# Moving gathered token rows into a quartered tile by sixteen transfers between partitions, without a copy in DRAM

## The chip, the cores and the metric

One Trainium2 chip, one of its cores. The metric is the device time of one execution in microseconds; the median of three runs of the kernel before is 671.84 us (670.88 to 672.2). Smaller is better. The engines are TensorE (PE in the profile; its weight loads stand apart as PEld), VectorE (DVE), ScalarE (ACT), GpSimd (POOL) and SyncE (SP), which here only issues transfers. A "q" behind an engine's name (SPq, DVEq) means its instruction queue: waits, branches and transfer issues.

## What is computed

Two layers one behind the other, all in 32-bit floats. The first is a linear attention with random features over 8 batches, 8 heads, 576 positions and 64 channels. Its output, 4608 rows of 512 values, goes through a mixture of experts in which each row is served by one of 8 experts:

```python
logits = x @ w_gate
expert_idx = np.argmax(logits, axis=1)
gate_w = probs[np.arange(N), expert_idx]      # probs: softmax of logits
for e in range(E):
    mask = expert_idx == e
    h = np.maximum(x[mask] @ w1[e], 0.0)      # 512 -> 1024
    out[mask] = gate_w[mask, None] * (h @ w2[e])   # 1024 -> 512
```

## The kernel before

Up to about 255 us the attention runs; it writes its rows, with the gate's weight behind each, to a DRAM tensor `token_rows`, and the routing (class `Routing`) makes index lists that sort the rows by expert. What follows is class `Experts`: it serves the sorted rows in chunks of up to 448 (three tiles of 128 rows and one of 64) that belong to one expert. The chunk in hand is counted by t. A first, early part of 256 rows is served before chunk 0. In this execution chunks 0 to 11 hold rows; moves and gathers are made for one or two more.

A step (`step`, line 1190) of chunk t consists of

- `layer1(t)`: four groups of two hidden blocks. Each group has 24 matmuls on TensorE, 96 in the chunk (line 1034), then `high_low` (line 1048): ScalarE makes the high part of the hidden block (line 1049), VectorE the low part (line 1050). Two PSUM buffers serve the four groups in turn, so the third group waits until VectorE has read the first.
- `layer2(t)`: up to 72 matmuls (line 932) or 16 for a half tile (line 1069) that make the output rows. Which tiles are done depends on the row count of the chunk, by branches in the instruction streams (`either`, line 1120; `three`, line 1108).
- `weigh(t+1)` and `gather(t+3)`: GpSimd copies the gate weights (line 981) and gathers the rows of a later chunk from `token_rows` into `xg[(t+3) % 2]`, four indirect transfers (line 975).
- `begin(t+1)` (line 1178): the move of chunk t+2 on SyncE, then the weight fetches if the expert changes (w2 at line 952, w1 at line 949, 2 MB each, both on SyncE), the split of w1 in a high and a low part on ScalarE (line 61) and VectorE (line 55), and `xrows(t+2)` (line 1013).
- `out2`: ScalarE scales the output rows (line 1151), GpSimd scatters them (line 1131).

The order on each engine is that of the code: it is scheduled by hand. Only at t = 1 `xrows(2)` stands within `layer1` (line 1091). In a step with a new expert `layer1` also splits w2, two blocks before each group.

The change is in `move` (line 989). The rows of a chunk lie in `xg`, one row on a partition. TensorE needs them turned. VectorE's transpose (line 1003) works on blocks of 32 by 32 within 32 partitions, so the columns must first be dealt out: the tile `xq` has in its q-th 32 partitions the q-th 128 columns of all rows, 32 rows to a block. `move` makes it by way of DRAM: two stores (lines 993 and 994) of 768 KB and 128 KB into `chunk_rows`, and four loads (line 996) of 224 KB, one for each quarter of the partitions, in pieces of 512 bytes. There is one `xq` and there are two `chunk_rows`; so the loads wait for the four transposes of the move before, and the stores don't. `xtrans` (line 998) writes the turned rows back into `xg`, `part` (line 1007) makes the high part on ScalarE (line 1010) and the low part on VectorE (line 55).

The framework sets the semaphores for all of this. A transfer that SyncE issues gets one of eight completion semaphores, in turn; the transfer that comes to a semaphore again waits for the one before on it.

In the profile the twelve moves are counted 1 to 12; move 1 is issued before chunk 0 starts.

Of the kernel before, what the change touches and what calls it, by code (L numbers as in the profile page):

```python
# [10 lines left out]
F32 = mybir.dt.float32  # L11
# [9 lines left out]
P = 128  # L21
Q = 32
B, H, S, D, M = 8, 8, 576, 64, 128
DM = H * D
# [12 lines left out]
A3 = 3  # L37
T3 = A3 * P
HT = P // 2
T4 = T3 + HT  # L40
# [795 lines left out]
class Experts:  # L836
# [7 lines left out]
    def __init__(self, tc, ctx, rt, xs, w1, w2, out, ident, ps):  # L844
        self.tc, self.nc, self.ctx, self.rt, self.ps, self.ident = tc, tc.nc, ctx, rt, ps, ident
        self.xs, self.w1, self.w2 = xs, w1, w2

        self.out = dram_disjoint_views(out, A3 + 1)
        cp = ctx.enter_context(tc.tile_pool(name="mo_a", bufs=1))
        self.w1s = cp.tile([P, self.NC, F], F32, name="w1s")  # L850
        self.w2s = cp.tile([P, self.NF, DM], F32, name="w2s")
        self.idx = cp.tile([P, NS], U32, name="idx")
        self.idx0 = cp.tile([P, 2], U32, name="idx0")
        self.flags = cp.tile([1, 5, NQ], I32, name="flags")
        self.xg = [cp.tile([P, A3 + 1, ROW], F32, name="xg")]
        self.clear = lambda: self.nc.gpsimd.memset(self.xg[0], 0.0)
        rt.setup()
        *rt.after[3], last = rt.head(4, self.idx0, self.flags)
        rt.late[5] = [last]
        self.x0 = cp.tile([P, self.NC, self.T2], F32, name="x0")  # L860
        self.bounce = [self.nc.dram_tensor(f"chunk_rows{i}", (T4, DM), F32, kind="Internal").ap() for i in range(2)]
        gt = cp.tile([P, 4 + 2 * A3], F32, name="gt")
        self.gt = [gt[:, i:i + 1] for i in range(4 + 2 * A3)]
        self.stored, self.now = 0, SimpleNamespace(r2=None, r3=None, fetch=None)
# [124 lines left out]
    def move(self, t):  # L989


        rows, x, dma = self.bounce[t % 2], self.xg[t % 2], self.nc.sync.dma_start
        dma(rows[:T3].rearrange("(a p) n -> p a n", p=P), x[:, :A3, :DM])
        dma(rows[T3:], x[:HT, A3, :DM])
        for q in range(4):
            dma(self.xq[q * Q:(q + 1) * Q], rows[:, q * P:(q + 1) * P].rearrange("(g i) n -> i g n", i=Q))

    def xtrans(self, t, a):

# [319 lines left out]
```

## Time and profile before

| | |
|---|---|
| median of three runs | 671.84 us (670.88 to 672.2) |
| the profiled execution, its own time | 675.24 us |
| its span, first to last instruction | 673.4 us |
| mean granted TensorE clock over the span | 0.991 of full speed |
| attention, from the span's start | to about 255 us |
| chunks 0 to 11 (TensorE, line 1034 and 932) | 268.1 to 666.1 us |

The profile is of one execution. "Busy" is time in which an engine computes; waits, branches and transfer issues don't count. A timeline lists start, duration, engine, line, operation, the tiles written and read, and in brackets how long the engine was idle before and what ended that. "remote" and "issue" there mean that no semaphore of this program's engines was found that ended the idle time.

### The profile page before, as it was taken

To read this page: it belongs to the slowest core of one execution; us is meant where nothing else is said; L and a number is where in the kernel's file an instruction comes from. 1 tells how busy PE (TensorE), PEld (TensorE's weight loads), DVE (VectorE), ACT (ScalarE), POOL (GpSimd) and SP (SyncE) were. 2 spreads that over 40 slices of the span, in tenths; PEclk is the share of its full clock that TensorE was granted. 3 is DMA by queue.
4 is the path that set the end of the run, shared out by engine and by line. 5 is a ranking of instruction groups with operands and counts; after the bars stand their busy time and mean duration, and the time that the engine had idled before them with its cause. 6 is when DMAs were issued, how large, how long until landed. Compare 5 with 4: busy or idle time off the path is not lost. (4 is left out here: it accounts for less than half of the span.)

```text
span 673.4 us, 19200 instructions
## 1 busy us (share of the span) xinstructions
PE 653.0 (97%) x6979; PEld 591.0 (88%) x6979; DVE 375.3 (56%) x755; ACT 359.8 (53%) x1089; POOL 280.5 (42%) x514
## 2 busy tenths in 40 slices
PE   8999999999999999999999999999997999999995
PEld 5999999999989987989898989898987989898984
DVE  4788888888888787732524184323267064614110
ACT  4999999999999956422222163212244143413111
POOL 5645546887788775152241304121222304031302
PEclk8999999999999999999999999999998999999998
DMA  7863926638390533759774256843268718530101
GB/s 216 230 186 105 278 84 202 192 104 263 77 336 27 181 103 85 200 167 308 186 195 83 84 159 151 251 127 87 67 216 215 217 53 230 197 91 18 35 1 56
DMA packets 95531, 102.07 MB, mean 152 GB/s; under 512 B 29454, under 2 KB 75534, under 8 KB 94736
## 3 DMA queue, kind: packets, MB, share of 16 engines
q1 hardware_dynamic: 87248, 80.84, 41.4%
q0 software_dynamic: 7440, 19.04, 9.3%
q8 instruction: 92, 1.51, 1.0%
q14 instruction: 63, 0.52, 0.3%
q10 hardware_dynamic: 688, 0.16, 0.1%
HBM read 74.77 MB, written 30.43 MB: 156 GB/s over the span
## 5 line engine op out<-in xcount | busy, mean ns | idle before, releaser
L1034 PE MATMUL p<-xb,w1p 128*128 128x384 f32 (+3 forms) x1152 | 195.8, 329 | 2.0 <-DVE hb L1050 1.9
L1034 PEld LDWEIGHTS p<-xb,w1p 128*128 128x128 f32 x1152 | 191.5, 188 | 5.9 <-DVE hb L1050 2.5
L932 PE MATMUL p<-w2p,hb 128*128 128x512 f32 x792 | 183.5, 392 | 3.6 <-PEq L1109 3.6
L932 PEld LDWEIGHTS p<-w2p,hb 128*128 128x128 f32 x792 | 149.6, 189 | 34.8 <-issue 3.8
L1131 POOL DMA_INDIRECT out_dram<-ys,idx x38 | 38.2, 1004 | 278.8 <-DVEq L1121 135.8
L1050 DVE SCALAR_TENSOR_TENSOR hb<-p,hb 128x768 fp32r<-128x768 f32 (+1 forms) x48 | 42.7, 890 | 191.5 <-ACT hb L1049 138.1
L1049 ACT ACTIVATE hb<-p 128x768 fp32r<-128x768 f32 (+1 forms) x48 | 36.4, 758 | 124.0 <-PE p L1034 92.3
L195 DVE TENSOR_REDUCE mx<-pp 128x8 f32<-128x1024 f32 x64 | 78.0, 1218 | 10.8 <-PE pp L189 9.0
L203 ACT ACTIVATE qp<-pp,mx 128x128 f32<-128x128 f32 x256 | 76.8, 432 | 0.0
L203 ACT ACTIVATE kp<-pp,mx 128x128 f32<-128x128 f32 x256 | 73.8, 382 | 5.2 <-DVE de L287 1.3
L189 PE MATMUL pp<-omt,th 64*128 64x128 f32 x1024 | 71.6, 280 | 0.2 <-ACT qp_-1_323 L203 0.2
L189 PEld LDWEIGHTS pp<-omt,th 64*128 64x128 f32 x1024 | 63.0, 190 | 0.3 <-ACT qp_-1_323 L203 0.3
L215 POOL TENSOR_TENSOR k<-kp 128x256 f32<-128x256 f32 x64 | 46.5, 726 | 25.2 <-ACT kp L203 19.5
L1151 ACT ACTIVATE ys<-p,gt 128x512 f32<-128x512 f32 x30 | 20.6, 688 | 59.0 <-PE p L932 36.6
L180 DVE COPY th<-tr 128x512 f32<-128x512 f32 x63 | 43.3, 687 | 6.1 <-PE tr L172 4.2
L278 PE MATMUL nu<-kva,qt 128*64 128x73 f32 x1008 | 46.0, 233 | 0.0
L247 ACT COPY qt<-t 128x512 f32<-128x512 f32 x64 | 41.8, 653 | 2.2 <-PE t L172 1.8
L975 POOL DMA_INDIRECT xg<-token_rows,idx x31 | 32.0, 1032 | 21.4 <-DVE xb L55 7.9
L278 PEld LDWEIGHTS nu<-kva,qt 128*64 128x64 f32 x1008 | 36.7, 136 | 4.2
L229 PE MATMUL kf<-kp,v 128*64 128x128 f32 x512 | 39.7, 275 | 0.4 <-issue 0.4
L975 POOL DMA_INDIRECT xgm<-token_rows,idx x28 | 28.2, 1008 | 7.6 <-issue 6.7
L216 POOL TENSOR_TENSOR ks<-k 128x128 f32<-128x128 f32 x64 | 29.2, 457 | 5.0
(382 smaller groups left out, 945.5 us busy)
## 6 DMA issues: line engine op xcount, KB each, us to landing
xq<-chunk_rows SPq DMA_DIRECT2D x48, 224.0 KB
w1s<-in_moe_w_dram SPq DMA_DIRECT2D x5, 2048.0 KB
w2s<-in_moe_w_dram SPq DMA_DIRECT2D x5, 2048.0 KB
v<-in_v_dram SPq DMA_DIRECT2D x32, 256.0 KB
token_rows<-x SPq DMA_DIRECT2D x8, 1024.0 KB
k<-in_k_dram SPq DMA_DIRECT2D x31, 256.0 KB
q<-in_q_dram SPq DMA_DIRECT2D x31, 256.0 KB
chunk_rows<-xgm SPq DMA_DIRECT2D x6, 768.0 KB
```

The lines of the kernel that those rows point to most:

```text
L180: self.nc.vector.tensor_copy(t.rearrange("p n (a t) -> p a n t", a=2), s[("tr", h)])
L189: nc.tensor.matmul(o[:, a, n, :], t[r, n, :], self.om[r], start=True, stop=True)
L195: self.nc.vector.tensor_reduce(out=mx, in_=s[("pp", h)], axis=AX.X, op=ALU.max, negate=True)
L203: self.nc.scalar.activation(o[:, j, :], p[:, a, 2 * n + i, :], AF.Exp, bias=mx[:, a, 2 * n + i:2 * n + i + 1])
L215: nc.gpsimd.tensor_tensor(out=k2, in0=kp[:, :2, :], in1=kp[:, 2:, :], op=ALU.add)
L229: nc.tensor.matmul(pkv[c * D:(c + 1) * D, :M], vv, kk, start=n < 2, stop=n > 2)
L247: self.nc.scalar.copy(qt.rearrange("p n (a t) -> p a n t", a=2), s[("t2", h)])
L278: nc.tensor.matmul(o[r, j, :], qt[:, j, r], kva[:, h if h >= 0 else 2 * j + a, :], start=True, stop=True)
L932: self.nc.tensor.matmul(p, x, w[:, c, :], start=c == 0 and x is h and w is self.w2h, stop=c == self.NF - 1 and x is l)
L975: self.nc.gpsimd.indirect_dma_start(out=self.xg[t % 2][:self.span(a), a, :], out_offset=None, in_=self.xs[:, :], in_offset=bass.IndirectOf ...
L1034: self.nc.tensor.matmul(o, w[:, c, k], x[:, c, :], start=i == 0, stop=i == len(ops) - 1)
L1050: self.nc.vector.scalar_tensor_tensor(out=l, in0=p, scalar=0.0, in1=h.bitcast(F32), op0=ALU.max, op1=ALU.subtract)
```

## The change

The two DRAM tensors go, and with them the two stores. In place of the four loads there are sixteen transfers from `xg` to `xq`, one for each 32 partitions g and each quarter of the columns q. Each takes the 32 partitions g of the source, of every row tile that has them (four tiles for g = 0 and 1, with the half tile; three for g = 2 and 3), and writes 32 partitions q, every fourth block. They are of 64 KB or 48 KB, again in pieces of 512 bytes, on SyncE as before.

```diff
-        self.bounce = [self.nc.dram_tensor(f"chunk_rows{i}", (T4, DM), F32, kind="Internal").ap() for i in range(2)]
...
-        rows, x, dma = self.bounce[t % 2], self.xg[t % 2], self.nc.sync.dma_start
-        dma(rows[:T3].rearrange("(a p) n -> p a n", p=P), x[:, :A3, :DM])
-        dma(rows[T3:], x[:HT, A3, :DM])
-        for q in range(4):
-            dma(self.xq[q * Q:(q + 1) * Q], rows[:, q * P:(q + 1) * P].rearrange("(g i) n -> i g n", i=Q))
+        x, dma = self.xg[t % 2], self.nc.sync.dma_start
+        for g in range(4):
+            n = A3 + (g < HT // Q)
+            for q in range(4):
+                dma(self.xq[q * Q:(q + 1) * Q, g:4 * (n - 1) + g + 1:4], x[g * Q:(g + 1) * Q, :n, q * P:(q + 1) * P])
```

## Rows read from the trace of the kernel before

**Rows 1.** The page, busy time of TensorE: us, share of the span, instructions.
```profile
PE 653.0 (97%) x6979; PEld 591.0 (88%) x6979; DVE 375.3 (56%) x755; ACT 359.8 (53%) x1089; POOL 280.5 (42%) x514
```

**Rows 2.** Timeline of TensorE, 268 to 673: start us, duration us, engine, line, operation.
```profile
...
339.99 16.84 PE L1034 MATMUL p<-xb,w1p 128*128 128x384 f32 x96
...
415.26 4.43 PE L1034 MATMUL p<-xb,w1p 128*128 128x384 f32 x24 [0.96 <-DVE hb L1050]
...
517.50 12.77 PE L932 MATMUL p<-w2p,hb 128*128 128x512 f32 x48 [3.56 <-PEq L1109]
...
572.65 4.45 PE L1034 MATMUL p<-xb,w1p 128*128 128x384 f32 x24 [0.93 <-DVE hb L1050]
```

**Rows 3.** Timeline of SyncE's issues, 255 to 673, moves 1, 2, 3, 6 and 9.
```profile
271.57 0.45 SPq L994 DMA_DIRECT2D chunk_rows<-xgm  x1
275.73 1.90 SPq L996 DMA_DIRECT2D xq<-chunk_rows  x4
...
308.31 0.40 SPq L952 DMA_DIRECT2D w2s<-in_moe_w_dram  x1
...
322.77 2.48 SPq L996 DMA_DIRECT2D xq<-chunk_rows  x4
...
406.48 2.16 SPq L996 DMA_DIRECT2D xq<-chunk_rows  x4
...
494.91 0.69 SPq L994 DMA_DIRECT2D chunk_rows<-xgm  x1
505.61 3.36 SPq L996 DMA_DIRECT2D xq<-chunk_rows  x4
```

**Rows 4.** Waits of SyncE's queue, whole span: total us, times, longest us.
```profile
SPq L996 <- DMA chunk_rows<-xgm: 46.6, 6, 11.2
...
SPq L996 <- DMA chunk_rows<-xg: 36.4, 6, 9.0
```

**Rows 5.** Waits of all engines, whole span: those for the quartered tile.
```profile
DVE xgm L1003 <- DMA xq<-chunk_rows: 6.1, 2, 5.1
```

**Rows 6.** Instructions of line 996: count, shortest, median and longest ns, first and last start.
```profile
L996 SPq DMA_DIRECT2D xq<-chunk_rows x48: 315/477/1943, 275.7 to 590.0; - x48
L996 SPq EVENT_SEMAPHORE  x24: 17/28/568, 275.6 to 588.1; - x24
```

**Rows 7.** Timeline of VectorE, 283 to 673.
```profile
321.51 0.64 DVE L1003 STREAM_TRANSPOSE xg<-xq 128x256 f32<-128x256 f32 x1
...
332.65 2.08 DVE L1003 STREAM_TRANSPOSE xgm<-xq 128x512 f32<-128x512 f32 x2 [5.12 <-DMA xq<-chunk_rows]
...
347.16 0.96 DVE L1050 SCALAR_TENSOR_TENSOR hb<-p,hb 128x768 fp32r<-128x768 f32 x1 [8.81 <-issue]
...
414.25 0.96 DVE L1050 SCALAR_TENSOR_TENSOR hb<-p,hb 128x768 fp32r<-128x768 f32 x1 [3.93 <-ACT hb L1049]
...
496.64 0.63 DVE L1003 STREAM_TRANSPOSE xg<-xq 128x256 f32<-128x256 f32 x1
...
514.84 0.68 DVE L1050 SCALAR_TENSOR_TENSOR hb<-p,hb 128x512 fp32r<-128x512 f32 x1
```

**Rows 8.** Timeline of ScalarE, first operations behind a wait, four steps.
```profile
346.24 0.81 ACT L1049 ACTIVATE hb<-p 128x768 fp32r<-128x768 f32 x1 [5.24 <-remote]
...
413.33 0.81 ACT L1049 ACTIVATE hb<-p 128x768 fp32r<-128x768 f32 x1 [4.90 <-remote]
...
473.38 0.81 ACT L1049 ACTIVATE hb<-p 128x768 fp32r<-128x768 f32 x1 [3.45 <-PE p L1034]
...
570.72 0.81 ACT L1049 ACTIVATE hb<-p 128x768 fp32r<-128x768 f32 x1 [4.99 <-remote]
```

**Rows 9.** Branches of line 1121 on TensorE's queue, whole span.
```profile
L1121 PEldq COMPARE_BRANCH  x198: 65/176/5002, 302.9 to 661.9; - x198
```

**Rows 10.** Busy us of each engine in two stretches, then clock, DMA engines' share, GB/s.
```profile
core 0: us, PE busy (x) PEld busy (x) DVE busy (x) ACT busy (x) POOL busy (x), PEclk, DMA share, GB/s
...
406.50:414.50 8.00, 7.80 (x45) 7.48 (x44) 2.50 (x4) 2.37 (x4) 4.86 (x9) 1.00 1.01 220
506.00:516.50 10.50, 7.87 (x64) 7.46 (x62) 6.19 (x10) 5.01 (x9) 3.44 (x4) 1.00 0.85 176
```

## The prediction

> **What bounds the kernel now.** I read the page's busy times first, then TensorE's timeline, then SyncE's queue (which issues the transfers in question), then what VectorE and ScalarE wait for behind them. TensorE is busy for 97% of the span [rows 1], so only its gaps can be won. Where the moves run it is one unbroken row of blocks but for three gaps: 0.96 us before 415.26, 3.56 us before 517.50 and 0.93 us before 572.65, together 5.45 us [rows 2]. Nothing else that this change touches can shorten the time: no TensorE instruction is added or removed.
>
> SyncE shows what a move is today: two stores, a wait, four loads. In move 1 the second store is issued at 271.57 and the first load at 275.73 [rows 3]: 4.2 us for the first leg when nothing lies ahead of it. Behind a 2 MB weight fetch it is more: 494.91 to 505.61 in move 9 [rows 3]; moves 3, 6, 7 and 11 repeat this. SyncE's waits for the first leg add up to 83.0 us in 12 moves [rows 4]. But SyncE is a queue, not the bound. Who waits for the result is VectorE, and only twice in twelve moves: 6.1 us in all, 5.1 at once [rows 5], that is move 3 before 332.65 and move 9 (0.98 us). In the other ten the quartered tile is ready before VectorE comes to it. None of TensorE's three gaps is such a wait: two are ended by VectorE's low part of a hidden block, one by a jump in TensorE's own program.
>
> **The change, part by part.** *Removed: the stores and the wait on them.* 24 stores and some 11 MB each way of DRAM traffic go (0.92 MB in 12 moves), with 83.0 us of SyncE's waiting. Worth nothing by itself, since SyncE's time is covered by TensorE's 16.5 us blocks; if that cover were gone it would be worth at most VectorE's 6.1 us.
>
> *Added: 16 issues for 4 loads.* One issue takes 0.315 to 1.943 us, median 0.477 [rows 6]. The new ones are smaller, and nothing shows one of that kind; I take the median: 16 x 0.477 = 7.6 us of SyncE per move, against 2.9 for today's six at the same price. What is queued behind them is the weight fetch of the same step. Move 2 has one right behind it, at 308.31 [rows 3]: it starts at most about 5 us later (7.6 - 2.9), and its first reader is the w2 split of the next expert, in the step whose hidden block stands at 413.33 [rows 8]. That covers it by more than 90 us; the other fetches wait for VectorE's splits anyway.
>
> *Moved: the wait for the quartered tile to be free.* The stores could go before that tile was free; now the first transfer waits for the four transposes of the move before. They end at 321.51 + 0.64 = 322.15 for move 3 and at 496.64 + 0.63 = 497.27 for move 9 [rows 7]. In move 3 that is 0.6 us before today's loads (322.77), so almost nothing is won there.
>
> *Completion.* The framework gives SyncE's transfers eight completion semaphores in turn, and a reused one is waited for first. So the sixteen go in two rounds of eight: the ninth waits until the first has landed. VectorE gains one or two wait instructions a move, GpSimd's gathers a few; a wait that is already met takes SyncE 0.03 us in the median [rows 6], and both engines are idle for longer in every step.
>
> *Move 3*, the tightest. Four loads took from 322.77 to 332.6, 9.8 us beside a gather. Sixteen start at 322.15. Lower bound, the same engine time: 332.0. Upper bound, one more round at the bare 4.2 us: 336.2. By issue the last one leaves at 322.15 + 7.6 = 329.8, and with 4.2 us it lands at 334.0. I take 333.8, 1.2 us later than now. VectorE then runs later by this, and ScalarE's copies behind it. TensorE feels it at the next hidden block: the block of 96 matmuls begins at 339.99, its third group of 24 at about 339.99 + 8.42 = 348.41 [rows 2], and needs VectorE's piece that ends at 347.16 + 0.96 = 348.12 [rows 7]. Slack 0.29 us. Cost: 1.2 - 0.3 = **0.9 us** (bounds 0 and 3.3).
>
> *Moves 6, 9, 11*: here the gaps are. Before its hidden block ScalarE idles 4.90 us to 413.33 and 4.99 us to 570.72, ended by "remote", not by matmuls, and 5.24 us to 346.24; in a step whose loads run elsewhere the same wait is 3.45 us and is ended by the matmuls [rows 8]. TensorE's longest jump is 5.0 us, against a median of 0.18 [rows 9]; it is the one that ends in the 3.56 us gap. In each of these four places the second leg of a move is on the DMA engines: their busy share is 1.01 from 406.5 to 414.5 and 0.85 from 506 to 516.5 [rows 10]. I read this as engines that wait after a jump for their next instructions, which come by the same DMA engines and take longer beside the move's small packets. The Trainium skill ("Runtime: NRT & Kernel Launch", section Instruction fetch mechanics) says that a taken jump out of the loaded pages waits for a DMA fetch; the rows of the jump agree, but do not name what is fetched.
>
> In the new kernel these transfers take the place of the first leg in the queue. Move 9: in line from 497.27 behind the same weight fetch, its first eight land near 505.6, where the first leg lands now; the second eight 4.2 us later, at 509.8. TensorE's jump near 512 then has quiet queues. It cannot gain all: VectorE's last piece ends at 514.84 + 0.68 = 515.52 [rows 7], so 517.50 - 515.52 - 0.05 = **1.9 us** goes (bounds 0 and 1.9; 0.05 us is the handover in 415.26 - 414.25 - 0.96, the same two engines). What is late next is that piece. Move 6: landed near 406.5 + 4.2 = 410.7 instead of 406.48 + 9.8 = 416.3, so about half of ScalarE's wait (408.4 to 413.33) lies clear of it. I take half of the 0.96 and, move 11 having the same form, half of the 0.93: **0.9 us** (bounds 0 and 1.9).
>
> Sum: -1.9 - 0.9 + 0.9 = -1.9 us. The profiled execution took 675.24 us, so 673.3 by its own time; it lies 3.4 us over the median of the runs, 671.84, against which the forecast is **669.9 us**.
>
> A rule speaks against this gain. The Trainium skill ("DMA: Bandwidth & Descriptors", Queues, rings and completion order) says that each DMA engine takes its queues in turn, packet by packet; by it an instruction load would wait for a packet or two, not for a move, the three gaps would stay, and the sum would be +0.9 us. The trace has four waits of 5 us beside a move's packets against 3.45, which no such short turn explains, but nothing that ties a load to a packet.
>
> **The rivals.** *Hidden anyway* (no change): ten of twelve moves have no waiter, and the three gaps are made by branches, weight splits and gathers, whose packets stay where they are. For it: GpSimd is issuing gathers and scatters for 4.86 of the 8 us from 406.5 [rows 10]. Against: the contrast in [rows 8]. Gains 0 to 0.9, move 3's cost 0 to 0.9: 671 to 673, middle **671.8**.
>
> *Two rounds too slow* (slower): sixteen transfers with eight in flight expose one landing per round, and a landing beside gathers and weights is no 4.2 us but up to the 9.8 of move 3. Place: move 3, the only one whose lateness reaches TensorE within 0.3 us. It decides from a landing at 332.9 on; with two rounds of 9.8 us it lands at 341.8, and the price is 341.8 - 332.6 - 0.3 = 8.9 us, **680.7**; with a quarter of the excess, 674. Other moves have more room: VectorE found ten of the twelve ready [rows 5]. [...] Against: eight transfers are half a move's bytes, enough to keep the engines full while one lands.
>
> The Trainium skill ("DMA: Bandwidth & Descriptors", Rules for kernel authors) has a harsher form: transfers under 64 KB are mostly overhead, about 2 us each. By it, one after another, sixteen would end at 354, and move 3 alone would cost 21 us. That they overlap is what today's four loads show, issued within 2.5 us.
>
> **How the numbers follow.** A measurement of this kernel can tell 0.2%, 1.3 us. Forecast (some of the three gaps closes): chance 0.45; hidden anyway: 0.34; too slow: 0.21. The forecast by itself runs from 671.84 - 3.8 = 668.0 to 671; the range takes in that, with 0.6 us of the runs' own spread below, the no-change case and the slow case up to 674.6: **667.4 to 674.6**. Faster 0.45, same 0.34, slower 0.21.
>
> **What would show it.** Right: no wait of SyncE for stores; sixteen issues of about 0.5 us; VectorE not waiting before the transposes of move 9; TensorE's 3.56 us gap near 1.6; ScalarE's "remote" waits of 4.9 us nearer 3.5. Wrong: the three gaps unchanged (hidden anyway), or VectorE's 5.1 us wait at move 3 grown past 7 and a new TensorE gap before the third group of the next block (too slow). A single issue of over 0.8 us would also make the forecast wrong.

## The result and the profile after

The kernel after took **675.83 us** (median of 11 runs, 673.42 to 678.93) against 671.92 us for the kernel before in the same measurement (11 runs, 670.16 to 672.87): a ratio of **1.006**, 95% interval 1.0044 to 1.0075, so 3.9 us slower. That is not the whole result. The same text, measured three more times later on two other occasions, took 666.57, 666.56 and 666.47 us, ratios of 0.992 to 0.993 to the kernel before beside it. (An occasion is one set of kernels run on one chip, with the kernel before among them.) No run of the one kind lies within 5 us of a run of the other. The larger part of what follows is about that difference; "after" alone means the first measurement.

Two lines of the page of the kernel before that did not stand above, of its DMA queues (packets, MB, share of 16 engines) and of DRAM traffic:

```profile
q1 hardware_dynamic: 87248, 80.84, 41.4%
...
HBM read 74.77 MB, written 30.43 MB: 156 GB/s over the span
```

The page of the kernel after, TensorE's busy time (against [rows 1]) and the same two lines:

```profile
PE 652.8 (97%) x6979; PEld 589.9 (88%) x6979; DVE 375.3 (56%) x755; ACT 360.4 (53%) x1089; POOL 281.4 (42%) x514
...
q1 hardware_dynamic: 83792, 69.84, 34.5%
...
HBM read 63.76 MB, written 19.42 MB: 123 GB/s over the span
```

The change does what it says: 11 MB each way of DRAM traffic are gone, and TensorE has the same work. Its timeline in the kernel after, the places with a gap of over 0.3 us, against the three of [rows 2]:

```profile
351.40 2.21 PE L1033 MATMUL p<-xb,w1p 128*128 128x384 f32 x10 [0.97 <-issue]
354.29 4.43 PE L1033 MATMUL p<-xb,w1p 128*128 128x384 f32 x24 [0.68 <-DVE hb L1049]
...
415.80 1.93 PE L1033 MATMUL p<-xb,w1p 128*128 128x384 f32 x10 [0.92 <-issue]
...
515.76 3.14 PE L1033 MATMUL p<-xb,w1p 128*128 128x256 f32 x24 [2.28 <-DVE hb L1049]
519.21 11.17 PE L931 MATMUL p<-w2p,hb 128*128 128x512 f32 x48 [0.32 <-PEq L1108]
...
541.52 3.78 PE L1033 MATMUL p<-xb,w1p 128*128 128x320 f32 x24 [0.58 <-DVE hq L1049]
...
573.52 4.43 PE L1033 MATMUL p<-xb,w1p 128*128 128x384 f32 x24 [0.83 <-DVE hb L1049]
```

The gap of 3.56 us at the jump (line 1109 before, 1108 now) has become 0.32, but 2.28 us stand just ahead of it, ended by VectorE's part of a hidden block; the gaps of chunks 4 and 9 (415 and 573) are about as long as they were; two at chunk 2 (351 and 354) and one at chunk 8 (541) are new. These seven add up to 6.6 us, against 5.45.

SyncE's issues in the kernel after (timeline, moves 3, 4, 6 and 9):

```profile
321.67 11.47 SPq L995 DMA_DIRECT2D xq<-xgm  x16
339.55 12.65 SPq L995 DMA_DIRECT2D xq<-xg  x16
...
401.51 11.64 SPq L995 DMA_DIRECT2D xq<-xg  x16
...
500.04 12.42 SPq L995 DMA_DIRECT2D xq<-xgm  x16
```

The same line's instructions (count, shortest, median and longest ns), to be held against [rows 6]:

```profile
L995 SPq DMA_DIRECT2D xq<-xgm x96: 585/600/2038, 270.9 to 569.4; - x96
L995 SPq DMA_DIRECT2D xq<-xg x96: 276/599/2136, 299.9 to 596.4; - x96
```

An issue takes 0.600 us in the median, not 0.477, and a move keeps SyncE for 10.4 to 12.8 us. What it waits for (against [rows 4], where the stores cost 83.0 us) is now VectorE and the gathers; there is no wait for a store, nor one for the first eight of the sixteen:

```profile
SPq L995 <- DVE xb L55: 63.0, 10, 14.5
...
SPq L995 <- DMA xg<-token_rows,idx: 19.7, 3, 14.5
```

All engines' waits in the kernel after, ScalarE's and that for the quartered tile (against [rows 5]):

```profile
ACT hb L1048 <- remote: 23.6, 5, 7.5
...
DVE xgm L1002 <- DMA xq<-xgm: 7.7, 1, 7.7
```

ScalarE's timeline in the kernel after, the steps of [rows 8] that wait, and the one before TensorE's 2.28 us:

```profile
352.35 0.81 ACT L1048 ACTIVATE hb<-p 128x768 fp32r<-128x768 f32 x1 [7.48 <-remote]
...
416.05 0.81 ACT L1048 ACTIVATE hb<-p 128x768 fp32r<-128x768 f32 x1 [3.97 <-remote]
...
514.30 0.60 ACT L1048 ACTIVATE hb<-p 128x512 fp32r<-128x512 f32 x1 [3.96 <-PE p L1033]
...
571.59 0.81 ACT L1048 ACTIVATE hb<-p 128x768 fp32r<-128x768 f32 x1 [4.82 <-remote]
```

and VectorE's, the tight move 3 (against 332.65 in [rows 7]):

```profile
334.77 2.07 DVE L1002 STREAM_TRANSPOSE xgm<-xq 128x512 f32<-128x512 f32 x2 [7.73 <-DMA xq<-xgm]
```

The gaps that VectorE ends (354, 516, 542, 574) follow a late ScalarE: a hidden block's high part starts late, VectorE's low part behind it, and TensorE finds no free PSUM buffer. The row at 514.30 names the matmuls, but those of that group had ended by about 504.69 + 2 x 8.79/3 = 510.6, so it is late by more than 3 us too. The gaps ended by "issue" (351, 416) are in the middle of a group, where TensorE waits for no semaphore that the profile shows.

What "remote" hides is in the trace's record of semaphore increments, which no view prints. ScalarE's hidden block waits for the semaphore that the last matmul of its group counts up; only TensorE's instructions count that one up. Each row is one wait of ScalarE (us):

| execution | ScalarE starts | idle before | TensorE's count recorded | last matmul of the group ends | count late by |
|---|---|---|---|---|---|
| before | 346.24 | 5.24 | 346.14 | 344.33 | 1.81 |
| before | 413.33 | 4.90 | 413.23 | 410.14 | 3.09 |
| before | 570.72 | 4.99 | 570.62 | 567.56 | 3.06 |
| after | 352.35 | 7.48 | 352.25 | 347.99 | 4.26 |
| after | 416.05 | 3.97 | 415.94 | 412.44 | 3.50 |
| after | 514.30 | 3.96 | 514.20 | 510.60 | 3.60 |
| after | 571.59 | 4.82 | 571.48 | 568.18 | 3.30 |
| after, second repeat | 347.80 | 3.35 | 347.69 | 347.67 | under 0.02 |

So ScalarE does start 0.1 us behind a semaphore of this program, and it is TensorE's. All 47 "remote" waits of the study are of this kind: they end 0.03 to 0.40 us behind such a count, which is recorded 1.5 to 4.8 us behind the end of the last matmul that makes one. The ends of matmuls are modelled in the profile, so it is not shown whether the matmul itself or only its count was late.

The profiled executions of before and after take nearly the same, 675.24 and 675.83 us, although their medians are 3.9 apart. One reason is TensorE's clock. After the 3.56 us gap the profiled execution of before ran at a lower granted clock in the stretch 517.5 to 530.3:

```profile
517.50:530.30 12.80, 12.80 (x50) 10.44 (x51) 4.70 (x8) 2.95 (x5) 1.03 (x1) 0.87 0.82 277
```

The mean is made of full speed and, in the first part of the stretch, 0.50, the lower of the two levels (1.2 GHz). The same block in the kernel after, behind gaps of 2.28 and 0.32:

```profile
519.20:530.40 11.20, 11.19 (x50) 9.29 (x51) 7.00 (x11) 3.43 (x6) 1.03 (x1) 1.00 0.67 222
```

A mean of 0.87 against 1.00: the block took 12.77 us [rows 2] against 11.17, so 1.6 us of the before's own time is the clock. Another is that this execution of before took longer than any of the eleven runs beside after (672.87 us at most).

### The profile page after: what moved, and what is told of

The parts are those of the page before. It is cut to its first block, busy times and chain, and to the rows that moved or that the text cites. A ratio compares the mean times of both kernels' runs of the same rounds, so it can differ in the third digit from the quotient of the medians.

```text
span 674.1 us, 19383 instructions
## 1 busy us (share of the span) xinstructions
PE 652.8 (97%) x6979; PEld 589.9 (88%) x6979; DVE 375.3 (56%) x755; ACT 360.4 (53%) x1089; POOL 281.4 (42%) x514
## 5 line engine op out<-in xcount | busy, mean ns | idle before, releaser
L1150 ACT ACTIVATE ys<-p,gt 128x512 f32<-128x512 f32 x30 | 20.5, 689 | 53.8 <-PE p L931 29.4
```

## Experiments

Ratios are to the kernel before, run beside each on the same chip, with 95% intervals; "gaps" are TensorE's from the first chunk on, added up in the profiled execution.

### Where the lateness of move 3 and the single quartered tile matter

**The kernel before once more**, nothing edited, to see how steady its gaps are.

> The kernel before, unchanged, for a second trace and for the clock of each run. If the 3.56 us gap and the drop of the clock behind it belong to the one profiled execution only (which lay 3.4 us over the median), this trace shows less than 4 us of TensorE gaps between 268 and 666 us, no second stretch at the lower clock, and a span near 670. If they belong to the kernel, gaps of some 5.5 us and a span near 673. Time 671.9 either way.

671.34 us, 0.9992 (0.9974 to 1.0009). Gaps 0.81 at 414.95, 0.73 at 511.18 and 2.83 at the jump. The gap at the jump came in both profiles of the kernel before; its size varies.

**Move 3 by way of DRAM**, the other eleven direct:

```diff
+        if t == 3:
+            rows = self.bounce
+            dma(rows[:T3].rearrange("(a p) n -> p a n", p=P), x[:, :A3, :DM])
+            dma(rows[T3:], x[:HT, A3, :DM])
+            for q in range(4):
+                dma(self.xq[q * Q:(q + 1) * Q], rows[:, q * P:(q + 1) * P].rearrange("(g i) n -> i g n", i=Q))
+            return
```

> The changed kernel with move 3 alone made as before, by two stores and four loads. Theory A (the loss is move 3's late landing, which VectorE and then TensorE wait for): VectorE's wait falls from 7.7 to about 5 us, the TensorE gaps of 0.97 and 0.68 us near 352 go, and the time is 671.5 to 673. Theory B (the pace: each of the sixteen issues takes 0.60 us, so every move lies on the DMA engines for 11 to 13 us instead of 5 to 8, and waits after jumps beside it grow): the time falls by 1 to 2 us at most, to 674 to 675, the gaps near 415, 517 and 541 stay.

678.14 us, 1.0083 (1.0054 to 1.0111). VectorE's wait for the tile fell from 7.7 to 5.6 us, as long as before the change, and yet TensorE's gap at chunk 2 grew. ScalarE in this kernel, and TensorE behind it:

```profile
350.01 0.81 ACT L1056 ACTIVATE hb<-p 128x768 fp32r<-128x768 f32 x1 [9.91 <-remote]
```
```profile
352.03 10.01 PE L1041 MATMUL p<-xb,w1p 128*128 128x384 f32 x48 [4.44 <-DVE hb L1057]
```

Neither theory foresaw a loss. It isn't move 3's lateness that costs here; it is ScalarE's wait, which ends with TensorE's count at 349.91, 2.3 us behind its last matmul.

**Two quartered tiles**, so that a move needn't wait for the transposes of the one before, measured on two occasions:

```diff
-        self.x0 = cp.tile([P, self.NC, self.T2], F32, name="x0")
+        self.x0t = cp.tile([P, A3 * self.NC + 2, P], F32, name="x0")
+        self.x0 = self.x0t[:, :2 * self.NC].rearrange("p (c h) t -> p c (h t)", c=self.NC)
...
-        self.xq = cr.tile([P, A3 * NC + 2, P], F32, name="xq")
+        self.xq = [cr.tile([P, A3 * NC + 2, P], F32, name="xq"), self.x0t]
```

> The changed kernel with two quartered tiles in turn, so that a move no longer waits for the transposes of the one before. Theory A: move 3 lands before VectorE comes to it, its wait of 7.7 us goes, and the time is 671 to 673. Theory B: moves still take 11 us each and lie beside other jumps; 673 to 676, and the gaps change places rather than go.

> The kernel with a second quartered tile once more, unchanged; it took 673.99 us (ratio 1.0034) in its first call, with ScalarE's waits at the first hidden block of a step as long as 8 us. If what holds the engines up is fixed by the text of the program and the order of its transfers, it comes out within 0.3% of that again (672 to 676 us). If it is fixed anew whenever a program is loaded on a chip, as three further copies of the kernel after suggest, it may come out at 666 to 668 us, with no ScalarE wait ended by "remote" and TensorE's gaps after 268 us under 2 us in all.

673.99 us, 1.0034 (1.0014 to 1.0054), and 673.35 us, 1.0048 (1.0024 to 1.0072). ScalarE waits on "remote" in both, 12.9 us in three waits and 22.3 us in five, and TensorE's gaps are 8.1 and 6.1 us. VectorE's wait for the tile fell to 0.6 us in both, which did not bring the time down, and this program came out the same on a second occasion.

### Are the sixteen issues, or their packets, the cause?

**No moves from the second on**, so that later chunks are computed from the rows that stand in the quartered tile:

```diff
+        if t > 1:
+            return
```

> The changed kernel with move 1 alone; moves 2 and on are left out, so the later chunks are computed from the rows of chunk 1 in the quartered tile. It bounds what all moves together cost. Theory B: without them the waits after jumps are short everywhere, the TensorE gaps fall under 2 us in all, and the time is 667 to 670.5. Theory A: what is gone is the wait in move 3 only, 671 to 672.5.

666.99 us, 0.9926 (0.9907 to 0.9945); gaps 0.7 us; one "remote" wait of 2.0 us. The three other kernels of this occasion (before, move 3 by DRAM, two tiles) had 11.3, 29.4 and 12.9 us of such waits and took 4 to 11 us longer.

**Sixteen transfers of one row tile each**, and **four instead of sixteen**, with the same number of packets:

```diff
-            n = A3 + (g < HT // Q)
+            n = A3 + (g < HT // Q) if t == 1 else 1
```

> The changed kernel with sixteen transfers a move, but from move 2 on of the first row tile alone: 512 packets of 512 bytes instead of 1792; the other tiles' rows in the quartered tile are left as they were. Issue theory (what delays the engines behind their jumps is that SyncE issues transfers for 10 us a move, few bytes or many): the gaps stay, 673 to 676. Packet theory (it is the packets on the DMA engines): with 2/7 of them the gaps shrink to about 2 us in all, 668 to 670.

```diff
-        for g in range(4):
+        for g in range(4 if t == 1 else 1):
```

> The changed kernel with four transfers a move from move 2 on (the first 32 partitions of the rows alone), of four row tiles each: the same 512 packets as in the kernel with sixteen small ones, by a quarter of the issues; the rest of the quartered tile is left as it was. Issue theory: 2.4 us of issues, the gaps go, 667 to 669, at least 3 us under the kernel with sixteen small ones. Packet theory: the same time as that one, 668 to 670.

666.05 us, 0.9929 (0.9904 to 0.9953), and 666.7 us, 0.9939 (0.9917 to 0.9961); gaps of 0.3 us each, no "remote" wait. With an issue at 0.589 us in the median although it carries 32 pieces and not 96 to 128, and a move at 10 to 14 us, the first of the two shows that sixteen issues alone cost TensorE nothing on this occasion. At this point it looked as if the packets did it. The next runs took part of that back.

**Without move 4**, and **without moves 6, 9 and 11**:

```diff
+        if t == 4:
+            return
```

> The changed kernel with move 4 left out (chunk 4 is computed from the rows of chunk 3 in the quartered tile). If move 4, which now lies beside the first layer of chunk 2, makes ScalarE's 7.5 us wait there, that wait falls to about 3 us, the gaps of 0.97 and 0.68 us near 352 go, and the time falls by 1.5 to 2.5 us to 673.3 to 674.5. If the wait there is move 3's lateness, nothing changes: 675 to 676.5.

```diff
+        if t in (6, 9, 11):
+            return
```

> The changed kernel with moves 6, 9 and 11 left out, those behind a weight fetch (chunks 6, 9 and 11 are computed from the rows of the chunk before in the quartered tile). If these three make the gaps near 415, 516 and 573, the gaps go and the time falls by 4 to 6 us, to 669.5 to 672; with move 4's share this is all of the 8.8 us that leaving out all moves won. If the gaps there are made by the w2 splits, they stay and the time falls by less than 2 us.

675.51 us, 1.0015 (0.9998 to 1.0033), and 673.24 us, 0.9986 (0.9966 to 1.0006). TensorE's gaps near 352 are gone without move 4, and the one near 573 is gone without move 11. The wait of ScalarE in the step of 573 falls with it, to 2.62 us ended by the matmuls. But ScalarE still waits in the other steps. Its timeline without move 4:

```profile
349.29 0.81 ACT L1050 ACTIVATE hb<-p 128x768 fp32r<-128x768 f32 x1 [5.22 <-remote]
```

and without moves 6, 9 and 11:

```profile
352.91 0.81 ACT L1050 ACTIVATE hb<-p 128x768 fp32r<-128x768 f32 x1 [8.17 <-remote]
...
417.52 0.81 ACT L1050 ACTIVATE hb<-p 128x768 fp32r<-128x768 f32 x1 [4.93 <-remote]
513.98 0.60 ACT L1050 ACTIVATE hb<-p 128x512 fp32r<-128x512 f32 x1 [2.19 <-remote]
```

SyncE's timeline of this last kernel, from 395 to 520, shows that no move runs in the steps of 417 and 514:

```profile
398.70 0.37 SPq L948 DMA_DIRECT2D w1s<-in_moe_w_dram  x1
423.70 0.39 SPq L951 DMA_DIRECT2D w2s<-in_moe_w_dram  x1
430.87 10.82 SPq L997 DMA_DIRECT2D xq<-xgm  x16
464.32 11.42 SPq L997 DMA_DIRECT2D xq<-xg  x16
496.83 0.37 SPq L948 DMA_DIRECT2D w1s<-in_moe_w_dram  x1
519.75 0.39 SPq L951 DMA_DIRECT2D w2s<-in_moe_w_dram  x1
```

A wait of 4.93 us with no move in flight, against 3.97 to 4.90 with one. So such a wait does not need a move in flight. That the moves have no part in it isn't shown: with all of them out, 2.0 us were left on an occasion where other kernels had 11 to 29, and in the step of 573 the wait fell with its move. At chunk 2 a move may lengthen one (5.22 without, 7.48 and 8.17 with move 4), and then TensorE feels it.

**The detour kept, its four loads cut into the same sixteen pieces** (the kernel before, edited), on two occasions:

```diff
-        for q in range(4):
-            dma(self.xq[q * Q:(q + 1) * Q], rows[:, q * P:(q + 1) * P].rearrange("(g i) n -> i g n", i=Q))
+        to = rows.rearrange("(g i) n -> i g n", i=Q)
+        for g in range(4):
+            n = A3 + (g < HT // Q)
+            for q in range(4):
+                s = slice(g, 4 * (n - 1) + g + 1, 4)
+                dma(self.xq[q * Q:(q + 1) * Q, s], to[:, s, q * P:(q + 1) * P])
```

> The kernel before, with each of its four loads from DRAM cut into the same four pieces as in the change: two stores and sixteen loads, the same 1792 packets. If the number of issues is what stretches a move and costs the time, a move's loads take 8 us or more of issues, TensorE's gaps grow, and the time is 674 to 680, over the kernel before by 3 us or more. If it is the source in the other partitions (sixteen or not), 671 to 673.

> Sixteen loads from DRAM behind the two stores, again, beside the changed kernel on one chip. If the number of issues costs the time, it is no faster than the changed kernel less 1 us. If the source in the other partitions does, it is 0.7 to 1.2% under the changed kernel and at or under the kernel before.

671.72 us, 0.9959 (0.9945 to 0.9974), and 669.31 us, 0.9965 (0.9949 to 0.9982). Its profiled executions differ: 674.75 us with 27.4 us of "remote" waits in seven, and 666.82 us with none, so one text can show either. The ratio is the same in both, since the kernel before was slower on the first occasion too (674.13 against 671.63 us). Its issues take 0.430 us in the median, from DRAM, against 0.600 from the other partitions; and it has no gap over 0.40 us at the jump, though both legs are there.

### The same kernel again

**The kernel after, unchanged**, on one occasion, and **twice on another**:

> The changed kernel again, on the same chip as the two beside it (the kernel before differs between chips by some 3 us, so kernels of different chips are compared by their ratios alone). Both theories: 1.004 to 1.008 of the kernel before.

> The changed kernel once more, one of two equal copies in this call. Its first measurement was 1.006 of the kernel before, the one beside the sixteen loads 0.992. Theory of the chip (the time of the same program differs by where it runs): this copy and its twin agree within 0.2%, at whatever ratio. Theory of the loading (each time that a program is loaded, its code and data come to lie otherwise, and waits behind jumps with it): the twins may differ by 0.5% or more on the same chip.

> The twin of the copy beside it, the same text. Theory of the chip: within 0.2% of it. Theory of the loading: it may differ by 0.5% or more. In both, where the time is near 667 the trace shows none of ScalarE's waits of 5 us and more ended by "remote" and less than 1.5 us of TensorE gaps; where it is near 675, both.

666.57 us, 0.9919 (0.9899 to 0.994); 666.56 us, 0.9931 (0.9912 to 0.995); 666.47 us, 0.9924 (0.9905 to 0.9942), where 1.004 to 1.008 was expected of the first. The two occasions were on different chips, and every engine's order of instructions is that of the first measurement. TensorE's timeline of the second repeat (the first of the pair), the blocks that answer to those above:

```profile
339.17 16.83 PE L1033 MATMUL p<-xb,w1p 128*128 128x384 f32 x96
...
499.88 11.67 PE L1033 MATMUL p<-xb,w1p 128*128 128x256 f32 x96
511.87 11.17 PE L931 MATMUL p<-w2p,hb 128*128 128x512 f32 x48 [0.32 <-PEq L1108]
```

ScalarE's:

```profile
352.01 0.81 ACT L1048 ACTIVATE hb<-p 128x768 fp32r<-128x768 f32 x1 [3.40 <-PE p L1033]
...
413.64 0.81 ACT L1048 ACTIVATE hb<-p 128x768 fp32r<-128x768 f32 x1 [1.19 <-PE p L1033]
```

SyncE's:

```profile
339.52 12.16 SPq L995 DMA_DIRECT2D xq<-xg  x16
...
398.37 11.40 SPq L995 DMA_DIRECT2D xq<-xg  x16
```

VectorE's wait for the quartered tile:

```profile
DVE xgm L1002 <- DMA xq<-xgm: 8.0, 1, 8.0
```

This is the sharpest pair of the study. Move 4 is issued from 339.52 on, 0.03 us from where it was (339.55), as slowly, and VectorE waits for move 3 a little longer (8.0 against 7.7). But no wait of ScalarE is ended by "remote": where it waited 7.48 us, the matmuls end each of its waits after 3.4. From the start of chunk 0's first block to that of chunk 11's second, after took 382.85 us (267.61 to 650.46) and this run 373.54 (267.29 to 640.83): 9.31 us. Taking the starts of neighbouring blocks in both timelines, all of it lies in the first layer of six chunks, where ScalarE waits for the counts: 2.40 in chunk 2 (339.49 to 358.56 against 339.17 to 355.84), 0.41 in 3, 1.66 in 4, 2.53 in 7, 0.83 in 8 and 1.45 in 9.

So the packets of the moves are not enough for ScalarE's waits, and a wait can come without one in flight. Which executions have them goes by the occasion, without exception in the twenty profiles ("remote" waits, us):

| occasion | kernels profiled, with their waits |
|---|---|
| first measurement | before 21.6, after 23.6 |
| chip 7 | before 11.3, move 3 by DRAM 29.4, two tiles 12.9, no moves 2.0 |
| chip 7, later | sixteen small, four, both gated orders: none |
| chip 0 | without move 4 29.7, without 6, 9 and 11 30.9, sixteen loads 27.4 |
| chip 6 | after, sixteen loads, stores kept: none |
| chip 10 | after, after, gated by DRAM: none |
| chip 12 | two tiles 22.3 |

On the occasions without waits TensorE's count came 0.02 us or less behind the last matmul of its group in all 480 groups of the first layer but one, where no count is recorded. So the two runs at 666 and 667 us with fewer packets prove nothing about packets: no kernel of their occasion waited, and the unchanged kernel can come out at 666.5 us. The run without any moves is another matter, since the kernels beside it did wait.

### What a late quartered tile costs, and another order

**The stores kept, and the direct transfers held until they have landed:**

```diff
+        dma(rows[:T3].rearrange("(a p) n -> p a n", p=P), x[:, :A3, :DM])
+        dma(rows[T3:], x[:HT, A3, :DM])
+        dma(self.landed[:1], rows[T3 - 1:T3, :8])
+        dma(self.landed[:1], rows[T4 - 1:T4, :8])
```

> The changed kernel with the two stores kept: SyncE waits for them by two loads of 32 bytes and then issues the sixteen transfers between partitions, which do not read what was stored. So they start when the sixteen loads from DRAM start, in the same number and sizes; only where they read differs. Source theory (packets read from the other partitions hold up the loads behind jumps more than packets read from DRAM): as slow as the changed kernel or slower, 1.004 to 1.012 of the kernel before. Start theory (the change costs by where in the step its transfers begin): 0.994 to 0.999, as the sixteen loads.

682.94 us, 1.0156 (1.013 to 1.0183), above what either theory allowed. It has no "remote" wait; this is the other cost, in the waits of VectorE for the tile:

```profile
DVE xgm L1008 <- DMA xq<-xgm: 28.8, 4, 18.3
...
DVE xg L1008 <- DMA xq<-xg: 10.3, 2, 6.6
```

and TensorE's gaps behind them:

```profile
331.28 15.93 PE L933 MATMUL p<-w2p,hb 128*128 128x512 f32 x60 [5.37 <-ACTq L1170]
...
362.34 10.34 PE L1039 MATMUL p<-xb,w1p 128*128 128x384 f32 x48 [6.78 <-DVE hb L1055]
```

At move 3 a wait of 8 us for the tile is hidden (the repeats above), one of 18 is not; the first gap stands behind a wait of 6.6 us in chunk 1, where the transposes lie within the first layer.

**A move two chunks ahead, let go from move 4 on by the chunk's last hidden block**, so that it runs beside the second layer; with two quartered tiles as above; once with the sixteen direct transfers, and on two occasions by way of DRAM:

```diff
-        if t + 1 < NCH:
-            self.move(t + 1)
...
+            if t + 2 < NCH:
+                self.nc.sync.dma_start(self.gate_out, self.hb[:1, 1, self.NF - 1, :8].bitcast(F32))
+                self.move(t + 2)
```

> The whole computation, with the sixteen transfers, two quartered tiles, and each move one step earlier in the program: from move 4 on it first waits (by a 32-byte transfer) for the hidden block of the chunk before to be finished, so that it runs beside the second layer's matmuls, where few jumps are. If the loss comes from moves beside the jumps of the first layer (both theories of it), the gaps go and the time is 667.5 to 670, under both kernels. If moves cost by their work wherever they lie, 672 to 676.

> The same order and the two tiles, with the way through DRAM (two stores and four loads) in place of the sixteen transfers. If placing is all, the same time as with sixteen, 667.5 to 670; if the sixteen issues cost more than the six even beside the second layer, 1 to 2 us faster than that.

> The kernel with two quartered tiles, the moves beside the second layer, and the way through DRAM, which was at 0.9971 of the kernel before. Since its moves keep clear of most jumps it should differ little from chip to chip or loading to loading: 0.994 to 0.998 again, its runs within 2 us of each other.

Direct: 670.39 us, 1.0000 (0.9985 to 1.0015), gaps 3.9 us, of them 1.37 behind a weight split and 2.05 behind a hidden block. By DRAM: 668.62 us, 0.9971 (0.9958 to 0.9985), and 668.45 us, 0.9962 (0.9948 to 0.9976), gaps 1.4 and 2.2 us. None has a "remote" wait, as no other kernel of their occasions has. The order by way of DRAM was faster than the kernel before both times, by 2.3 and 3.0 us; the kernel after, where its ScalarE isn't held up, is faster still.

## Why the prediction was right or wrong

The forecast was 669.9 us, within 667.4 to 674.6; the first measurement lies 1.2 us above the range and the three later ones 0.8 us or more below it.

**The bound** held: what was lost was lost by TensorE in its first layers. Of the 9.31 us between after and its repeat 6.5 are gaps in the records; the rest lies between matmuls that are recorded as running.

**Removed.** SyncE's waits for stores went, and were worth nothing by themselves, as said.

**Added: 16 issues.** Mis-sized. The median of the loads from DRAM, 0.477 us, was taken for transfers between partitions, which take 0.600: 9.6 us at the median instead of 7.6, and 10.4 to 12.8 us with the longer ones. The w2 fetch behind move 2 left at 311.45, 3.1 us later than before, within the 5 forecast.

**Completion** in two rounds of eight did not show: SyncE has no wait for one of its own sixteen, so the first had landed by the time that eight issues (4.8 us at the median) were out. The rival *two rounds too slow* falls with it, though its signs came: VectorE's wait at move 3 grew to 7.7 us, a gap opened in the next block, and the longest single issue took 2.1 us. In the repeats VectorE waits as long, single issues take 2.0 us at the longest, and there is no such gap; the signs did not tell this rival from what happened. Its harsher form, 2 us for each transfer one after another, did not come either: the sixteen of move 3 left within 11.5 us, and the transposes began 13.1 us after the first. (The Trainium skill, "DMA: Bandwidth & Descriptors", has this figure in its section Anatomy of one DMA, for transfers that GpSimd issues, and not in the rules that the prediction names.)

**Move 3.** The transposes began at 334.77, 2.1 us later and not 1.2, since the issues take longer. The price of 0.9 us was wrong in kind. The 0.29 us of slack was counted from VectorE's piece ending at 348.12, and that piece was late because ScalarE ahead of it had waited 5.24 us [rows 8], the last 1.81 of them for TensorE's count. Where ScalarE isn't held up there is more room: in the runs at 666.5 us VectorE waits 8.0 to 8.8 us and TensorE has no gap there.

**Moves 6, 9, 11.** This is the step that failed: "I read this as engines that wait after a jump for their next instructions, which come by the same DMA engines and take longer beside the move's small packets." The four places were the right ones, and the waits do hold TensorE up. But for ScalarE the reading is wrong: [rows 8] were taken as "ended by 'remote', not by matmuls", and each of them ended 0.1 us behind TensorE's count for the group (346.14, 413.23, 570.62), which was 1.8 to 3.1 us late. From the count to ScalarE's start it is the same 0.1 us as in the repeat, so ScalarE stood ready and waited for TensorE. What held TensorE's own jump of 5.0 us [rows 9], no run shows. Nor were the packets that carry instructions slower: behind 268 us those of the page's queue q8 took 1.09 us in the median and 2.09 at the longest in the first measurement, 1.13 and 1.70 in the second repeat, which has no such wait. And the contrast on which the reading rested, 5 us beside a move against 3.45 elsewhere, was at most a part of the cause: with moves 6, 9 and 11 out a wait stays (4.93 us to 417.52), and with the moves in place they can be gone. The clear time was not won either: issuing alone went on to 413.1 in move 6 and 512.5 in move 9, where the transfers were to have landed by 410.7 and 509.8. Of the 1.9 us at the jump 0.96 came (3.56 against 2.28 + 0.32), of the 0.9 us at moves 6 and 11 nothing. The jump's own gap closed as forecast and more, but it also closed with both legs kept (0.40 us and less), so the reason given for it isn't confirmed.

The Trainium skill ("DMA: Bandwidth & Descriptors", Queues, rings and completion order) lets each DMA engine take its queues in turn, packet by packet. The prediction set it aside on the strength of that contrast; with the contrast that weak, nothing here speaks against it. The Trainium skill ("Runtime: NRT & Kernel Launch", Instruction fetch mechanics) says that a taken jump out of the loaded pages waits for a fetch. No run here shows that this is what was lost: ScalarE waited for TensorE's count, the same jumps go with a wait of 7.48 us in one execution and of 3.4 in another, and no row names a fetch.

**The new gaps at chunk 2**, 0.97 and 0.68 us, go with both move 4, which the prediction put at nothing without a reason, and a ScalarE that is held up: in these runs they are gone without the one, and without the other.

**What stays open.** Why TensorE's counts come late, in the first measurement and not in the three later ones, with the same instructions in the same order. It goes by the occasion and not by the text: all kernels of an occasion have such waits or none has, also different ones, and two copies agreed to 0.1 us. Chip 7 had them on one occasion and not on a later one, though with other kernels, so the chip alone would not explain it; a place in memory that each program gets for itself would have to fall alike for all programs of an occasion. One rival was not tested, the recording of the trace: in the executions with waits fewer increments are recorded, for the kernel after 8603 of all semaphores against 10634 to 10690 in the repeats. Whether the recording holds TensorE up, or the same thing holds up both, is not shown. Nor is it shown where the 5 us come from by which the repeats are faster than the kernel before, since that was profiled only on occasions with waits. For that reason the honest result is two numbers: 0.6% slower on the one occasion with waits, 0.7 to 0.8% faster on the two without.

## What to carry to other kernels

Before a transfer is blamed for an engine's wait, leave that transfer out and look at the wait, not at the total time: here the total fell and a wait stayed. When the profile finds no cause for a wait, look up the semaphores that the instruction waits for and when each was counted up: here that showed that "remote" was TensorE. A difference under 1% should be measured on more than one occasion, and experiments on one occasion compared with each other, since this kernel moved by 9 us with nothing changed and all kernels of an occasion went the same way. Issues are priced by their kind: from DRAM and from other partitions are two prices, and sixteen of the dearer kind cost TensorE nothing here (gaps of 0.3 us with sixteen small transfers), since what stood behind them in the queue could wait.

## What the runs showed of the hardware that was not expected

- A transfer from partitions to partitions takes SyncE 0.600 us to issue with 96 to 128 pieces and 0.589 us with 32; the same pieces from DRAM take 0.430 us. The number of pieces hardly matters.
- TensorE's count for a group of matmuls is recorded 0.02 us or less behind the end of the last one on some occasions, and up to 4.8 us behind it on others, in every kernel profiled there. ScalarE's waits for it came to 23.6 us in one profile of a program and to nothing in another of the same program, and the two differ by 9.3 us of TensorE's time.
- Behind a gap of TensorE of 3.56 us the granted clock of the next 12.8 us was 0.87 in the mean, and the block there took 1.6 us longer; behind gaps of 2.28 and 0.32 us it stayed at 1.00. The length of one gap does not settle it: with two tiles it stayed at 1.00 behind a gap of 2.87 us (before 351.53), and in the gated order it fell to 0.50 behind one of 2.05 us (before 538.26).
